# Windowed attention into a SwiGLU block: TensorE's order of work from block 2 on, written out instead of planned

## The chip, the cores and the metric

The kernel runs on one core of a Trainium2 chip. The metric is the device time of one execution in microseconds (us). TensorE is called PE below, VectorE DVE, ScalarE ACT, GpSimd POOL and SyncE SP, as in the profile.

## The reference

The inputs q, k and v have 8 batches, 8 heads, 576 positions and a head size of 64. Attention looks back over a window of 128 positions, with a linear bias per head, and its output, as 4608 tokens of 512 numbers, goes through a gated feed-forward layer with 1536 hidden units.

```python
scores = q @ k.T / sqrt(64)
scores = where((rel >= 0) & (rel < 128), scores - slope[h] * abs(rel), -1e9)
x = softmax(scores) @ v                  # 4608 x 512
out = (silu(x @ w_gate) * (x @ w_val)) @ w_out
```

## The kernel before

Two streams of work share the engines.

**The feed-forward stream** (`ffn`) goes through nine blocks of 512 tokens. In blocks 0 to 5 there are 12 slices m of 128 hidden units, each in two half-steps: the gate product (`pg`, four matmuls of 512 columns, line 398), then ACT's tanh (416) and DVE's `uu` (417); the val product (`pv`, 398), then DVE's `hT` (428). Both take a PSUM bank of the tag `gv`, of which there are three. Blocks 6 to 8 form gate and val from seven products of half size in place of eight (`seven_steps`, line 624), 42 half-steps to a block.

The output projection of block n runs inside block n+1. From block 1 on it is done by `strassen`: two halves t of the columns of tokens, seven products each of six 256-wide matmuls (533), which add up in the two halves X and Y of one bank `po`, and in a bank `p2` for the second product. ACT and DVE copy X and Y out between the products (544 to 576, 537). The set `AT` names the half-steps of a block behind which one such product is written.

The products need sums of quarters of `hT` (`sums`, four DVE operations for each of three chunks c, lines 486 to 489), and of the output weights (`weight_sums`). The seven-step blocks need like sums of the gate and val weights (`gate_val_weight_sums`, 598 to 601) and of the attention output (`x_sums`). `at_once` writes such a list of operations in one go. `later` is a list from which operations are taken off one by one; before the change only the seven-step blocks use it.

**The attention stream** (`attention`) goes through 36 units, nine for each pair of batches. For a unit i it writes:

- `transposes_to`: K and Q transposed, from rank 11 on by DMAs that SP issues;
- `scores(i + 1)`: products of 64 rows (`ps` line 279, `psc` line 314), evicted by ACT with an exponential (285, 318), then multiplied with a mask by DVE (291, 322). One unit's products take all four banks of the tag `a`;
- `weighted(i)`: the product with v (`av`, line 346) in two halves, each in a bank `a`, then DVE's reciprocal and multiply into `x` (348, 349);
- `loads_to` and `ahead`: DMA loads by POOL, some units in advance, and further transposes;
- `x_transposed(i)`: `x` turned into `xT`, up to unit 23 by PE (`px`, line 372) and ACT, later by a DMA. For the units 13 to 23 it is written while the scores of two units on are being written.

Each `yield` of `attention` is one attention step. `ffn` yields sizes (1.0 for a half-step, 0.75 for a product of `strassen`), whose running sum is `step`. Block 2 begins behind step 60, block 6 behind step 198. After each yield of `ffn`, `everything` writes attention steps until their number reaches `target`, and until the units that the block six steps ahead needs are done (`ready`).

**Who sets the order.** A planner orders each engine's instructions by a cost model of its own, except inside `manual_schedule`, where the named engines keep the order of the source. The first tiles are written so for PE, DVE and ACT. From `step >= FIXED_FROM` on it holds for PE alone; the other engines stay with the planner.

Of the kernel before, what the change touches and what calls it, by code (L numbers as in the profile page):

```python
# [19 lines left out]
X_DMA_FROM = 24  # L20
# [11 lines left out]
SEVEN_FROM = 6  # L32
SILU_AT = 7
SECOND = 5.5
RATE = 6.7
FIXED_FROM = 198.0
LATE = 13


# [12 lines left out]
def kernel(  # L52
# [15 lines left out]
    NMB = DFF // P  # L68
# [96 lines left out]
    last = len(units) - 1  # L165
# [318 lines left out]
    def four_sums(a11, a12, a21, a22, s2, s3, s4):  # L484

        return [lambda: nc.vector.tensor_sub(s3, a11, a21),  # L486
                lambda: nc.vector.tensor_add(a21, a21, a22),
                lambda: nc.vector.tensor_sub(s2, a21, a11),  # L488
                lambda: nc.vector.tensor_sub(s4, a12, s2)]

    def at_once(fs):
        for f in fs:
            f()

    def sums(n, c):

        if n not in hsum:
            hsum[n] = [spool.tile([P, HM, 256], FP16, name=f"S{i}", tag=f"S{i}") for i in (2, 3, 4)]
        lo, hi = slice(2 * c, 2 * c + 2), slice(HM + 2 * c, HM + 2 * c + 2)
        a11, a12 = hT[n][:, lo, 0:256], hT[n][:, hi, 0:256]  # L500
        a21, a22 = hT[n][:, lo, 256:512], hT[n][:, hi, 256:512]
        s2, s3, s4 = (t_[:, lo, :] for t_ in hsum[n])
        return four_sums(a11, a12, a21, a22, s2, s3, s4)
# [90 lines left out]
    def gate_val_weight_sums(u):  # L594

        cols = slice(2 * u * P, (2 * u + 2) * P)
        t1, t2, t3, t4 = tsum[u] = t_homes[4 * u:4 * u + 4]
        return [lambda: nc.vector.tensor_sub(t1, V1[:, :, cols], G1[:, :, cols]),
                lambda: nc.vector.tensor_sub(t3, V2[:, :, cols], V1[:, :, cols]),
                lambda: nc.vector.tensor_sub(t2, V2[:, :, cols], t1),  # L600
                lambda: nc.vector.tensor_sub(t4, G2[:, :, cols], t2)]

    def x_sums(n):

        a11, a12 = xT[n][:, 0:HK, 0:256], xT[n][:, HK:NKB, 0:256]
        a21, a22 = xT[n][:, 0:HK, 256:512], xT[n][:, HK:NKB, 256:512]
        s2, s3, s4 = xsum[n] = spare[3 * (n % 2):3 * (n % 2) + 3]
        return four_sums(a11, a12, a21, a22, s2, s3, s4)

    later = []  # L610
# [86 lines left out]
                    of[which[0]][name](which[1])  # L697
                yield n, 7 * u + k, name, which

    AT = {2, 3, *range(5, 10), *range(11, 18)}  # L700

    def ffn():

        for n in range(NBLK):
            if n > 1:
                parts = chain(strassen(n - 1, 0), strassen(n - 1, 1))
            if n == 1:
                for j in range(PRE):
                    for _ in project(0, j, ps_f, "po", 1):
                        yield 1.0  # L710
            if n == SEVEN_FROM:
                break
            for m in range(NMB):
                for half, _ in enumerate(gate_val(n, m)):
                    yield 1.0
                    if n > 1 and 2 * m + half in AT:
                        next(parts)
                        yield 0.75
                if n == 1:
                    if m in (4, 6, 8, 10):  # L720
                        for _ in project(0, m // 2 - 2, ps_f, "po", 1):
                            yield 1.0
                    if m in (4, 6, 8):
                        weight_sums(m // 2 - 2)
                if n > 0 and m >= 9:
                    at_once(sums(n, m - 9))
                if n + 1 == SEVEN_FROM:
                    if m == SILU_AT:
                        attention_ends()
                        by_silu.update((n, i) for i in range(m + 1, NMB))  # L730
                    if m in (SILU_AT + 1, SILU_AT + 2):
                        at_once(gate_val_weight_sums(m - SILU_AT - 1))
                    if m == NMB - 1:
                        at_once(gate_val_weight_sums(2))
                        at_once(x_sums(n + 1))
            if n > 1:
                assert next(parts, 0) == 0
        ends = [strassen(NBLK - 1, t) for t in range(2)]
        final = ()
        for n, k, name, which in seven_steps():  # L740
            if k == 0 and n > SEVEN_FROM:
                assert next(parts, 0) == 0
                parts = chain(strassen(n - 1, 0), strassen(n - 1, 1))
            if n == SEVEN_FROM and k in (3, 10, 17):
                later.extend(gate_val_weight_sums(3 + k // 7))
            yield 0.5
            if k % 3 == 1 and k < 42:
                next(parts)
                yield 0.75
            if k == 20 and n + 1 < NBLK:  # L750
                later.extend(x_sums(n + 1))
            if k == 35:
                later.extend(sums(n, 0))
            if name == "fourth" and which is not None and which[1] > 3:
                if which == (NBLK - 1, 5):
                    at_once(final)
                else:
                    later.extend(sums(which[0], which[1] - 3))
            if n == NBLK - 1 and k == 40:
                final = sums(n, 2)  # L760
                later.append(final.pop(0))
            for _ in range(2 if len(later) > 4 or k >= 39 or k < 7 else 1):
                if later:
                    later.pop(0)()
            if n == NBLK - 1 and k == 41:
                next(ends[0])
                yield 0.75
        assert next(parts, 0) == 0 and not later

        for t in (1, 0, 1, 0, 0, 0, 1, 0, 0, 1, 1, 1, 1):  # L770
            next(ends[t])
            yield 0.75
# [22 lines left out]
    def run(steps):  # L795
        for fs in steps:
            for f in fs:
                f()
            yield
# [34 lines left out]

    def attention():

        waiting = set()
        transposes_to(need[FIRST])
        for _ in run(scores(FIRST)):
            yield FIRST  # L840
        for i in range(FIRST, last + 1):
            behind = LATE <= i < X_DMA_FROM
            if i < last:
                transposes_to(need[i + 1])
                for n, _ in enumerate(run(scores(i + 1))):
                    yield i - (i - 1 in waiting)
                    if n == 2 and i - 1 in waiting:
                        x_transposed(i - 1)
                        waiting.discard(i - 1)
            weighted(i)  # L850
            yield i
            loads_to(i + 7)
            ahead(i)
            yield i
            if behind:
                waiting.add(i)
                yield i
                yield i
                continue
            x_transposed(i)  # L860
            yield i
            yield i + 1
# [63 lines left out]
    def everything():  # L926
        nonlocal done
        base = 0
        busy(WARM)
        with tc.manual_schedule(engines=ENGINES[MANUAL]):  # L930
            first_tiles()
            done = FIRST
            steps = progress(ffn())
            while (at := next(steps)) < ALONE:
                if at == 2.0:
                    nc.scalar.copy(idm2, idm)
                if at in (1.0, 3.0, 4.0):
                    later_masks(2 * (1, 3, 4).index(at) + 2, 2)
        fixed = ExitStack()
        for step in steps:  # L940
            if step >= FIXED_FROM and fixed is not None:
                fixed.enter_context(tc.manual_schedule(engines=ENGINES["pe"]))
                fixed, held = None, fixed
            if step == MASKS_AT:
                make_masks()

            b1 = 24 + 3 * PRE

            lead = LEAD if done < X_DMA_FROM - 2 else LEAD + 4
            blk = (0 if step + LEAD < b1 else 1 if step + LEAD < 60  # L950
                   else min(NBLK - 1, 2 + int((step + lead - 60) // 34.5)))
            if step < b1:

                target = base + 1.25 * max(0, step - ALONE) + 1.5 * max(0, step - 16)
            elif step < 60:
                target = base + 32 + SECOND * 8 * (step - b1) / (60 - b1)
            else:
                target = base + 32 + SECOND * 8 + (step - 60) * RATE * 8 / 34.5
            while (n_att < target or done < ready[blk]) and att_step():
                pass  # L960
        held.close()
# [32 lines left out]
```

The softmax here doesn't subtract the row's maximum and nothing guards it: scores larger than these inputs give would overflow.

## Time and profile before

| | |
|---|---|
| median of 4 runs | 348.69 us (348.07 to 349.44) |
| the profiled execution | 349.44 us |
| its span, first to last instruction | 347.6 us |
| PE busy | 333.9 us (96%) |
| DVE busy | 278.0 us (80%) |
| ACT busy | 207.4 us (60%) |
| granted TensorE clock | 1.000 |

Busy times are unions of the recorded spans. Matmuls are pipelined: the record of one overlaps that of the next, so a PE that is busy all the time can still lose time between matmuls, which shows in the spacing of their starts. The idle time of an engine in front of an instruction is put down to what released it, by its semaphores. A few matmul records are missing.

### The profile page before, as it was taken

The numbers are of one execution on the slowest core, as the hardware profiler recorded it, in microseconds if no ns is written. First come the engines' busy times: TensorE is split into PE (matmuls) and PEld (weight loads), VectorE is DVE, ScalarE is ACT, GpSimd is POOL, SyncE is SP. The second block draws the span as 40 slices with busy tenths as digits, with TensorE's granted clock in tenths as the row PEclk, the third lists the DMA queues.
The fourth block names the chain that finished last, engine by engine and source line by source line (L and its number), as shares of the span: only waits on it lengthen the run. The fifth ranks groups of instructions, "written<-read, shape, count | busy, mean of one in ns | idle before, by whom it ended". The sixth has DMA issues, their size and how long they took to land.

```text
span 347.6 us, 7798 instructions
## 1 busy us (share of the span) xinstructions
PE 333.9 (96%) x2983; PEld 219.3 (63%) x2983; DVE 278.0 (80%) x652; ACT 207.4 (60%) x412; POOL 108.2 (31%) x134
## 2 busy tenths in 40 slices
PE   7999988999999999999999999999999999999995
PEld 4484444454456655566566554566688878878884
DVE  6578885999788699878999799999955875775583
ACT  3758674565655765574754646556467666766750
POOL 8967485257566564536511000000000000000000
PEclk9999999999999999999999999999999999999999
DMA  9999999999999999999994420221201101011014
GB/s 151 170 180 185 142 160 171 109 136 131 140 165 158 181 154 165 155 166 190 151 177 78 75 79 15 32 77 31 78 0 62 62 1 62 2 61 62 1 62 122
DMA packets 158981, 37.37 MB, mean 108 GB/s; under 512 B 147296, under 2 KB 154592, under 8 KB 158944
## 3 DMA queue, kind: packets, MB, share of 16 engines
q0 software_dynamic: 117280, 18.62, 80.5%
q1 hardware_dynamic: 40976, 17.64, 28.7%
q10 hardware_dynamic: 688, 0.62, 0.6%
q8 instruction: 23, 0.38, 0.5%
q14 instruction: 14, 0.11, 0.1%
HBM read 37.91 MB, written 9.44 MB: 136 GB/s over the span
## 4 chain that ended last, share of the span: by engine, by line
PE 63%; DVE 20%; DMA 8%; ACT 4%; issue 3%; POOL 1%; POOLq 0%; ACTq 0%; DVEq 0%
PE po L533 13%; PE pg L398 12%; PE pv L398 11%; PE gX L624 6%; DMA va<-in_v_dram 3%; PE av L346 3%; DMA wo_sb<-in_moe_w_out_dram 3%; PE ps L279 3%; PE gY L624 3%; DVE hT L428 3%; PE p L533 2%; DVE uu L417 2%; DMA qn<-in_q_dram 2%; DVE S L486 2%; PE po L452 2%
## 5 line engine op out<-in xcount | busy, mean ns | idle before, releaser
L398 PE MATMUL pv<-xT,wv_sb 128*128 128x512 f16 (+2 forms) x320 | 76.8, 358 | 0.4 <-DVE hT L428 0.2
L398 PE MATMUL pg<-xT,wg_sb 128*128 128x512 f16 (+2 forms) x320 | 76.2, 358 | 0.5 <-DVE hT L428 0.2
L416 ACT ACTIVATE tt<-pg 128x512 f16<-128x512 f32 (+2 forms) x70 | 41.5, 592 | 40.8 <-PE pg L398 39.4
L285 ACT ACTIVATE ex<-ps 128x512 f16<-128x512 f32 x96 | 50.5, 607 | 16.6 <-PE ps L279 16.5
L417 DVE SCALAR_TENSOR_TENSOR uu<-tt,pg 128x512 f16<-128x512 f16 (+2 forms) x69 | 46.0, 667 | 11.1 <-ACT tt L416 11.0
L428 DVE TENSOR_TENSOR hT<-uu,pv 128x512 f16<-128x512 f16 (+2 forms) x70 | 46.7, 667 | 3.4 <-PE pv L398 1.8
L398 PEld LDWEIGHTS <-wg_sb 128*128 128x128 f16 x320 | 28.5, 98 | 25.2 <-issue 3.3
L398 PEld LDWEIGHTS <-wv_sb 128*128 128x128 f16 x320 | 28.5, 98 | 24.5 <-issue 2.7
L191 POOL DMA_DIRECT2D kn<-in_k_dram x39 | 33.3, 857 | 33.3 <-DMA kT<-kn 24.5
L533 PEld LDWEIGHTS <-hT 128*128 128x128 f16 x384 | 36.5, 98 | 9.2 <-issue 1.1
L185 POOL DMA_DIRECT2D va<-in_v_dram x40 | 34.1, 858 | 22.5 <-PE av L346 15.6
L191 POOL DMA_DIRECT2D qn<-in_q_dram x39 | 33.3, 857 | 23.0 <-DMA qT<-qn 8.6
L291 DVE TENSOR_TENSOR ex<-ex,m_reg 128x1024 f16<-128x1024 f16 x42 | 28.9, 690 | 5.6 <-ACT ex L285 5.4
L533 PEld LDWEIGHTS <-S 128*128 128x128 f16 x288 | 27.3, 98 | 9.3 <-issue 1.8
L349 DVE TENSOR_TENSOR x<-av,rec 128x256 f16<-128x256 f32 x72 | 28.9, 420 | 0.5
L533 PE MATMUL po<-T,S 128*128 128x256 f16 x192 | 26.5, 273 | 1.3 <-DVE S L488 1.0
L533 PE MATMUL po<-T,hT 128*128 128x256 f16 x192 | 26.2, 273 | 0.0
L318 ACT ACTIVATE exc<-psc 128x512 f16<-128x512 f32 x40 | 21.4, 610 | 7.6 <-PE psc L314 7.6
L676 DVE TENSOR_TENSOR hT<-s,v 128x512 f16<-128x512 f16 x18 | 7.6, 424 | 21.4 <-ACT s L675 21.4
L346 PEld LDWEIGHTS <-ex 128*128 128x128 f16 x384 | 17.5, 97 | 5.2 <-issue 0.9
L346 PE MATMUL av<-va,ex 128*128 128x65 f16 x384 | 19.3, 193 | 0.3
L279 PE MATMUL ps<-qT,kT 64*128 64x256 f16 x192 | 18.4, 272 | 0.6 <-DVE osb L537 0.2
(134 smaller groups left out, 538.7 us busy)
## 6 DMA issues: line engine op xcount, KB each, us to landing
out_dram<-osb SPq DMA_DIRECT2D x32, 256.0 KB, 3.5
va<-in_v_dram POOLq DMA_DIRECT2D x32, 128.0 KB, 9.6
qn<-in_q_dram POOLq DMA_DIRECT2D x31, 128.0 KB, 7.4
kn<-in_k_dram POOLq DMA_DIRECT2D x31, 128.0 KB, 7.8
wo_sb<-in_moe_w_out_dram POOLq DMA_DIRECT2D x2, 768.0 KB, 9.3
wg_sb<-in_moe_w_gate_dram POOLq DMA_DIRECT2D x4, 256.0 KB, 8.0
wv_sb<-in_moe_w_val_dram POOLq DMA_DIRECT2D x4, 256.0 KB, 8.4
wg_sb<-in_moe_w_gate_dram POOLq DMA_DIRECT2D x1, 512.0 KB, 9.0
```

The source lines that it names most:

```text
L185: nc.gpsimd.dma_start(va[rank][p0:p1, :, 0:D], src)
L191: nc.gpsimd.dma_start(t_[p0:p1], src)
L285: nc.scalar.activation(e[:, o:o + 2, :], banks[q4][par], AF.Exp, scale=scale)
L291: nc.vector.tensor_mul(e[:, o, :], e[:, o, :], reg[:, o, :])
L346: nc.tensor.matmul(av[:, j, :], w, val, start=(n == 0), stop=(n == len(todo) - 1))
L349: nc.vector.tensor_mul(x[:, 4 * half:4 * half + 4, :], av[:, :, 0:D], rec.broadcast_to([P, 4, D]))
L398: nc.tensor.matmul(ps[:, c0:c1], w[:, kb, ms], xT[n][:, kb, c0:c1], start=(kb == 0 and c0 == 0), stop=(kb == NKB - 1 and c1 == 512), skip_ ...
L416: nc.scalar.activation(tt, pg[:, c0:c1], AF.Tanh, scale=0.5)
L417: nc.vector.scalar_tensor_tensor(out=uu, in0=tt, scalar=one if (n, m) == PIN else 1.0, in1=pg[:, c0:c1], op0=ALU.add, op1=ALU.mult)
L428: nc.vector.tensor_mul(hT[n][:, m, c0:c1], acted[(n, m)][1][:, c0:c1], pv[:, c0:c1])
L533: nc.tensor.matmul(dst, a[:, m, cols], b[:, m, :], start=(start and m == 0), stop=(m == HM - 1), skip_group_check=True)
L624: nc.tensor.matmul(dst[:, i, :], w[:, kb, c0 + i * P:c0 + (i + 1) * P], a[:, kb, :], start=(start and i == 0 and kb == 0), stop=(i == 1 an ...
```

## The change

- `FIXED_FROM` goes from 198.0 to 60: PE follows the source from the end of block 1 on.
- `AT` spreads the 14 products of `strassen` over the half-steps 1 to 22 of a block; before they lay in the half-steps 2 to 17.
- `sums` from the last chunk of block 1 on, `x_sums` and the `gate_val_weight_sums` of block 5 go into `later`. In blocks 2 to 5 one operation is taken off behind each half-step, two when more than three wait. The third of the weight sums moves to block 6, and `x_sums` is queued at slice 7 instead of being written at slice 11.
- `target` behind step 60 becomes 84 + (step - 57) * 54 / 34.5; before it was 76 + (step - 60) * 53.6 / 34.5.
- For units from 13 on, `weighted(i)` is written behind the third step of `scores(i + 1)` instead of behind the last, and `x_transposed` behind the weighted sums of the next unit.

```diff
--- before.py
+++ after.py
@@ -32,8 +32,8 @@
 SEVEN_FROM = 6
 SILU_AT = 7
 SECOND = 5.5
-RATE = 6.7
-FIXED_FROM = 198.0
+RATE = 54.0
+FIXED_FROM = 60
 LATE = 13
 
 
@@ -697,7 +697,7 @@
                     of[which[0]][name](which[1])
                 yield n, 7 * u + k, name, which
 
-    AT = {2, 3, *range(5, 10), *range(11, 18)}
+    AT = {1, 3, 4, 6, 8, 9, 11, 12, 14, 16, 17, 19, 20, 22}
 
     def ffn():
 
@@ -716,6 +716,10 @@
                     if n > 1 and 2 * m + half in AT:
                         next(parts)
                         yield 0.75
+                    if n > 1:
+                        for _ in range(1 + (len(later) > 3)):
+                            if later:
+                                later.pop(0)()
                 if n == 1:
                     if m in (4, 6, 8, 10):
                         for _ in project(0, m // 2 - 2, ps_f, "po", 1):
@@ -723,16 +727,15 @@
                     if m in (4, 6, 8):
                         weight_sums(m // 2 - 2)
                 if n > 0 and m >= 9:
-                    at_once(sums(n, m - 9))
+                    (at_once if n == 1 and m < 11 else later.extend)(sums(n, m - 9))
                 if n + 1 == SEVEN_FROM:
                     if m == SILU_AT:
                         attention_ends()
                         by_silu.update((n, i) for i in range(m + 1, NMB))
                     if m in (SILU_AT + 1, SILU_AT + 2):
-                        at_once(gate_val_weight_sums(m - SILU_AT - 1))
-                    if m == NMB - 1:
-                        at_once(gate_val_weight_sums(2))
-                        at_once(x_sums(n + 1))
+                        later.extend(gate_val_weight_sums(m - SILU_AT - 1))
+                    if m == SILU_AT:
+                        later.extend(x_sums(n + 1))
             if n > 1:
                 assert next(parts, 0) == 0
         ends = [strassen(NBLK - 1, t) for t in range(2)]
@@ -741,8 +744,8 @@
             if k == 0 and n > SEVEN_FROM:
                 assert next(parts, 0) == 0
                 parts = chain(strassen(n - 1, 0), strassen(n - 1, 1))
-            if n == SEVEN_FROM and k in (3, 10, 17):
-                later.extend(gate_val_weight_sums(3 + k // 7))
+            if n == SEVEN_FROM and k in (1, 3, 10, 17):
+                later.extend(gate_val_weight_sums(2 + (k + 4) // 7))
             yield 0.5
             if k % 3 == 1 and k < 42:
                 next(parts)
@@ -834,29 +837,34 @@
 
     def attention():
 
-        waiting = set()
+        waiting = []
         transposes_to(need[FIRST])
         for _ in run(scores(FIRST)):
             yield FIRST
         for i in range(FIRST, last + 1):
-            behind = LATE <= i < X_DMA_FROM
+            late = i >= LATE
             if i < last:
                 transposes_to(need[i + 1])
                 for n, _ in enumerate(run(scores(i + 1))):
-                    yield i - (i - 1 in waiting)
-                    if n == 2 and i - 1 in waiting:
-                        x_transposed(i - 1)
-                        waiting.discard(i - 1)
-            weighted(i)
-            yield i
+                    yield i - len(waiting)
+                    if n == 2 and late:
+                        weighted(i)
+                        yield i - len(waiting)
+            if not late or i == last:
+                weighted(i)
+                yield i
             loads_to(i + 7)
             ahead(i)
-            yield i
-            if behind:
-                waiting.add(i)
+            yield i - len(waiting)
+            if late and i < X_DMA_FROM:
+                if waiting:
+                    x_transposed(waiting.pop(0))
+                waiting.append(i)
                 yield i
                 yield i
                 continue
+            while waiting:
+                x_transposed(waiting.pop(0))
             x_transposed(i)
             yield i
             yield i + 1
@@ -955,7 +963,7 @@
             elif step < 60:
                 target = base + 32 + SECOND * 8 * (step - b1) / (60 - b1)
             else:
-                target = base + 32 + SECOND * 8 + (step - 60) * RATE * 8 / 34.5
+                target = 84 + (step - 57) * RATE / 34.5
             while (n_att < target or done < ready[blk]) and att_step():
                 pass
         held.close()
```

## The prediction

> **What bounds the kernel now.** I read the page first. TensorE (PE) is busy nearly all the time, at full granted clock, so a gain has to come out of the gaps between matmuls.
>
> ```profile
> span 347.6 us, 7798 instructions
> PE 333.9 (96%) x2983; PEld 219.3 (63%) x2983; DVE 278.0 (80%) x652; ACT 207.4 (60%) x412; POOL 108.2 (31%) x134
> DVE  6578885999788699878999799999955875775583
> PEclk9999999999999999999999999999999999999999
> ```
>
> The third and fourth lines are tenths of 40 slices of 8.7 us. DVE (VectorE) stands at 9 from slice 23 to 28, about 200 to 250 us, and lower after. So I looked at blocks 2 to 5, about 103 to 247 us, in windows of 12 us, three to a block; the columns are the window, its length, the busy time of PE, PEld, DVE, ACT, POOL, then clock, DMA share, GB/s.
>
> ```profile
> 127.00:139.00 12.00, 11.94 (x100) 6.41 (x99) 11.64 (x27) 7.60 (x16) 5.64 (x7) 1.00 1.80 155
> 139.00:151.00 12.00, 11.99 (x115) 7.40 (x114) 10.07 (x26) 6.72 (x13) 6.63 (x8) 1.00 2.07 159
> 151.00:163.00 12.00, 12.00 (x111) 7.57 (x109) 8.79 (x19) 7.93 (x17) 5.75 (x7) 1.00 1.60 178
> 163.00:175.00 12.00, 11.51 (x97) 6.29 (x96) 12.00 (x31) 7.32 (x15) 5.76 (x7) 1.00 2.10 169
> 223.00:235.00 12.00, 12.00 (x112) 7.24 (x112) 11.91 (x29) 6.29 (x14) 0.00 (x0) 1.00 0.24 67
> 235.00:247.00 12.00, 11.87 (x116) 7.66 (x116) 11.99 (x35) 6.50 (x13) 0.00 (x0) 1.00 0.30 78
> ```
>
> DVE swings: 8.8 of 12 in mid block 3, 12.0 in its last third, saturated in all of block 5. ACT (ScalarE) is at 58% over the twelve windows (83.6 of 144).
>
> Then PE's waits, first in this stage (103 to 247), then in the stage that is already in source order (247 to 341): total, times, longest.
>
> ```profile
> PE po L533 <- DVE osb L537: 0.5, 2, 0.3
> PE psc L314 <- DVE x L349: 0.5, 1, 0.5
> PE po L533 <- ACT p5s L561: 0.3, 1, 0.3
> PE pg L398 <- DVE hT L428: 0.2, 1, 0.2
> ```
> ```profile
> PE po L533 <- DVE S L488: 1.0, 2, 0.7
> PE gX L624 <- DVE v L667: 0.6, 3, 0.2
> ```
>
> These count only idle time after the modelled end of a pipelined matmul and so understate. The timeline of PE shows the real spacing by its starts:
>
> ```profile
> 164.97 0.61 PE L279 MATMUL ps<-qT,kT 64*128 64x256 f16 x8
> 165.51 0.83 PE L533 MATMUL po<-T,hT 128*128 128x256 f16 x6
> 166.18 1.03 PE L398 MATMUL pg<-xT,wg_sb 128*128 128x512 f16 x4
> 171.37 0.56 PE L314 MATMUL psc<-qT,kT 64*128 64x128 f16 x11
> 172.42 0.39 PE L314 MATMUL psc<-qT,kT 64*128 64x128 f16 x5 [0.49 <-DVE x L349]
> ```
>
> Six 256-wide matmuls take 0.67 from start to next start, 0.109 each; 512-wide ones 0.215; likewise 0.029 for 128x65, 0.055 for 128x128, 0.054 and 0.0275 for the 64-row ones of 256 and 128 columns. The starts from 103.0 on cover 144.2 us with 350, 324, 352, 44, 104 and 112 of these: 75.3 + 35.3 + 10.2 + 2.4 + 5.6 + 3.1 = 131.9. So blocks 2 to 5 hold 12.3 us that are not streaming. I split them by the pair of neighbours: 14 gaps of over 0.16 us make 4.5 (the 0.67 at 171.7 is the largest), and entering a group of 64-row matmuls costs 0.10 before it and up to 0.15 behind it, 0.24 for each of 26 entries, 6.3. The rest, 1.5, is crumbs. From 247 to 340 the same count leaves five gaps, 2.4 us: two on the sums S (1.3), three on v (1.1).
>
> **The change part by part.** No matmul is added or removed; all that can move is the 12.3 us.
>
> *Source order.* (a) The score groups of units 14 to 35 are written as 22 unbroken groups, against 26 entries in the trace: 4 x 0.24 = -1.0. Ends: 0 (others break up) and -1.4 (the two breaks of 0.22 inside groups go too). (b) The waits. What a written order costs here is shown by 247 to 340: without the waits on S, which come of sums in fours before a product, 1.1 in 93 us; over 144 us that is 1.65, and scaled by DVE's share (130.6 of 144 against 63.8 of 93) 2.2. With the waits on S it would be 3.7. I take 2.2, since the change takes the sums one or two per half-step.
>
> *Pacing.* I worked the target formula through by hand. Before, the rule on `ready` pushes attention to count 80 at step 54, the target passes 80 only at step 63, and unit 14's scores come there. After, the target at step 60 is 88.7: nine yields run at once (scores 14 around the weighted sums of unit 13), and from there attention is about 8 steps ahead: unit 20's scores at step 87.25 instead of 95.5, the last unit done at 172.75 instead of 182.5. A step is 1.07 us here (block 2 begins at 101.3, the first seven-step product at 249.4: 148 us for 138 steps). The nine yields cost PE a wait: the first half of the weighted sums needs a bank that the first eviction frees, 0.22 (half the group) + 0.60 after the group's start, while PE is through at 0.43: 0.4. With a tanh (0.49) ahead of it 0.9, and the next group of scores may wait as much: 0.4 to 1.7, I take 0.8 by the nearer row. So waits 4.5 -> 2.2 + 0.8 = 3.0: -1.5.
>
> *Spread products and single sums.* Counted from the order as written, with DVE's back-to-back spacing (0.60 for gate, val and mask, 0.335 for sums and x, 0.09 for rec), a block asks 30 to 34 us of DVE for 34 to 39 of PE. By thirds of blocks the demand over PE's is 0.74, 0.77, 1.09 / 0.68, 0.75, 1.20 / 0.73, 0.78, 1.15 / 0.79, 0.69, 1.26 before, the last third carrying twelve sums (4.0 us) and no products of PE in its last six half-steps. After: 0.82, 0.85, 0.92 / 0.89, 0.80, 0.87 / 1.04, 0.77, 1.00 / 0.92, 0.57, 0.76. This is why I trust (b). One spacing gets tighter: the seventh product of one half and the first of the next are one half-step apart; the copy between them (0.38) lies under a gate of 0.86. Costed at nothing; with a tanh ahead of the copy the cover is gone and it costs 0.1 four times.
>
> *Moved sums.* Eight sums more run in block 6 (2.7 us of DVE) and S of block 5 is written in its steps 1 to 4, used in step 7, 3.3 us later; DVE is at 26.7 of 36 there. Nothing. The waits on S at 281 and 310 belong to blocks 7 and 8, whose order is not touched, and stay.
>
> *Transposes and loads* go with attention: the SP queue and POOL keep their own order. Q of rank 19 landed at 112.9 for scores at 125.5; 8 steps earlier they stand at about 117. Some 4 us are left, so nothing, if the landing keeps its time.
>
> Sum: -1.0 - 1.5 = -2.5 against the profiled execution of 349.4 (span 347.6 and 1.8 around it): 346.9. That execution is 0.75 above the median of the runs, 348.7, so the forecast is **346.2**. Its own ends: every wait and four to six breaks gone, -5.9, 342.8; waits at 3.7 + 1.7 and no groups saved, +0.9, 349.6.
>
> **Two rules of the Trainium skill that speak against it.** The trace: while the group at 171.37 waited for x, the val product behind it did not start. "PSUM — Partial Sum Buffer", section "Engine vs sequencer instructions", says that matmuls start and complete in program order; a row agrees, and by the rule every wait that the writer did not see is paid whole, as in the first rival. The trace: the granted clock is 1.00 in all twelve windows with waits up to 0.67 us. "TensorE: Matmul & The Clock Gate", section "A second HAM failure mode: psum-queue depth-cycling", says that frequent micro-idling can make the clock gate oscillate; by that page's window of 3.4 us, one at half clock would add an estimated 1.7 us. No row here shows it, and the sum leaves it out.
>
> **The rivals.**
> 1. *Slower: weighted sums meet late evictions.* In the new order each weighted group comes a half-step and mostly one product after the next unit's scores, 0.86 + 0.66 us; its second half starts some 0.4 later and needs the second eviction, ready 1.30 after the scores' start, 1.79 with a tanh ahead. About half a microsecond is left. If ACT falls one more slot (0.48) behind, PE waits some 0.35 in each of 22 units: +7.7, 353.9. For it: the order cannot adapt, and banks of `ps_a` are four, all taken by one score group. Against: ACT at 58%. 0.17.
> 2. *Slower: K and Q come late.* The SP queue waits mostly for loads, the DMA share is near 2 until 187 us. If landings slip by more than the 4 us left at units 18 to 20, PE stands 2 to 6 us once: 348 to 352, say 350. 0.08.
> 3. *No change: the scheduled order is nearly the written one already*, or DVE (130.6 of 144) sets the pace: the waits only change names, 348.7. Until unit 20 the trace agrees to 2 us with the written order; in block 5 it does not, unit 35's scores run at 234.8 where the order has them near 224. 0.13.
>
> **How the numbers follow.** The forecast has 0.62. A measurement of this kernel can tell about 0.3%, 1.05 us. Faster by more than that takes waits below some 4.4 us in all with the groups saved: 0.62; within it 0.13; slower 0.25, the two slower rivals. The range takes in the forecast's ends, the second rival and the milder half of the first: 342.8 to 352.0, leaving out about 0.15.
>
> **What would show it.** Right: DVE in windows of 12 us no longer at 12.0 in the last third of a block and below 10 in the second half of block 5; 22 entries into 64-row groups; gaps over 0.16 us from 100 to 247 near 3 us, one of them at scores 14; the last scores some 10 us earlier; the first seven-step product (249.4 now) near 247. Wrong: waits of `av` on evictions of `ps` by the dozen (rival 1), of `ps` on DMA of kT or qT (rival 2), or the same 4.5 us under other names (rival 3).

## The result, and the profile after

The changed kernel takes 347.96 us (median of 46 runs, 347.08 to 348.98) against 349.06 us before (70 runs): a ratio of 0.9973, 95% interval 0.9967 to 0.9980. That is 1.1 us faster; 2.5 us had been forecast. The direction was right, the size was less than half.

The page of the changed kernel, its span, its engines and the rows of DVE and of the granted clock:

```profile
span 346.6 us, 7787 instructions
...
PE 330.0 (95%) x2983; PEld 218.9 (63%) x2983; DVE 277.3 (80%) x652; ACT 207.2 (60%) x412; POOL 108.2 (31%) x134
...
DVE  6578885999798669988899999999855875775583
...
PEclk9999999999999999999999999999999999999999
```

The same work, the same clock. DVE's row is not flatter where it was meant to be: slices 20 to 27 (counted from 0), about 173 to 243 us, all stand at 9. The windows of 12 us (columns as before: length, busy PE, PEld, DVE, ACT, POOL, clock, DMA share, GB/s) say the same:

```profile
127.00:139.00 12.00, 10.90 (x94) 6.22 (x91) 10.31 (x27) 7.30 (x15) 6.49 (x8) 1.00 1.98 145
...
163.00:175.00 12.00, 12.00 (x130) 7.67 (x129) 10.56 (x24) 8.04 (x16) 6.26 (x8) 1.00 2.21 141
175.00:187.00 12.00, 11.99 (x105) 6.91 (x104) 12.00 (x31) 7.39 (x15) 0.89 (x1) 1.00 1.54 209
187.00:199.00 12.00, 11.83 (x108) 7.08 (x106) 11.82 (x30) 6.56 (x13) 0.00 (x0) 1.00 0.24 67
199.00:211.00 12.00, 12.00 (x102) 7.05 (x101) 11.26 (x28) 6.43 (x14) 0.00 (x0) 1.00 0.12 24
211.00:223.00 12.00, 11.21 (x110) 6.69 (x109) 12.00 (x29) 7.29 (x15) 0.00 (x0) 1.00 0.23 67
223.00:235.00 12.00, 11.36 (x116) 7.32 (x114) 12.00 (x32) 6.49 (x12) 0.00 (x0) 1.00 0.21 60
235.00:247.00 12.00, 12.00 (x74) 6.97 (x72) 10.98 (x30) 3.58 (x8) 0.00 (x0) 1.00 0.10 29
```

The last third of block 3 is relieved (10.56 for 12.00), but late block 5 hardly (12.00 and 10.98 for 11.91 and 11.99). PE, on the other hand, now loses busy time in places where it lost almost none: 10.90 from 127 (11.94 before), 11.36 from 223 (12.00 before). PE's waits from 93 to 250 us (total, times, longest) tell on what:

```profile
PE po L533 <- DVE osb L537: 1.9, 3, 1.1
PE psc L314 <- ACT exc L318: 0.8, 1, 0.8
PE p L533 <- ACT ex L285: 0.7, 1, 0.7
PE av L346 <- ACT ex L285: 0.7, 2, 0.5
```

The worst of them, in the timeline of PE and DVE:

```profile
129.40 0.82 PE L533 MATMUL po<-T,S 128*128 128x256 f16 x6
...
130.00 0.68 DVE L417 SCALAR_TENSOR_TENSOR uu<-tt,pg 128x512 f16<-128x512 f16 x1
130.06 1.03 PE L398 MATMUL pg<-xT,wg_sb 128*128 128x512 f16 x4
...
130.71 0.69 DVE L428 TENSOR_TENSOR hT<-uu,pv 128x512 f16<-128x512 f16 x1
...
131.32 0.42 DVE L349 TENSOR_TENSOR x<-av,rec 128x256 f16<-128x256 f32 x1
...
131.74 0.40 DVE L537 SCALAR_TENSOR_TENSOR osb<-po,p5s 128x256 f32<-128x256 f32 x1
...
132.19 0.49 PE L533 MATMUL po<-wo_sb,S 128*128 128x256 f16 x3 [1.10 <-DVE osb L537]
```

The fifth product (`po<-T,S`) is followed one half-step later by the sixth (`po<-wo_sb,S`). They write different halves, X and Y, of one tile of one bank. The sixth waits for DVE's copy of X (`osb<-po,p5s`), and that copy is queued behind `uu`, `hT` and an `x`: it starts at 131.74, while PE had run out of other work at about 130.9. The next product in the written order waits, and with it all that is written behind it.

Counted by the starts of matmuls as in the prediction, but over the whole stage (from the end of block 1's projection at 93.5 or 93.3 to the first seven-step product), the streaming of the matmuls takes 142.6 us in both. Above that lie 13.3 us before and 12.4 after. The gaps of over 0.16 us, called gaps from here on, rose from 5.1 to 6.4 us; the small rest, with the entries into 64-row groups down from 27 to 22, fell from 8.2 to 6.0. The first seven-step product starts at 248.3 instead of 249.4, and everything behind it takes as long as before.

### The profile page after: what moved, and what is told of

Same layout as the page of the kernel before. It is cut to its first block, busy times and chain, and to the rows that moved or that the text cites. A ratio compares the mean times of both kernels' runs of the same rounds, so it can differ in the third digit from the quotient of the medians.

```text
span 346.6 us, 7787 instructions
## 1 busy us (share of the span) xinstructions
PE 330.0 (95%) x2983; PEld 218.9 (63%) x2983; DVE 277.3 (80%) x652; ACT 207.2 (60%) x412; POOL 108.2 (31%) x134
## 4 chain that ended last, share of the span: by engine, by line
PE 55%; DVE 25%; DMA 9%; ACT 5%; issue 4%; POOL 1%; ACTq 0%; DVEq 0%; POOLq 0%
PE po L533 12%; PE pg L398 11%; PE pv L398 9%; PE gX L624 6%; DVE uu L417 3%; DMA wo_sb<-in_moe_w_out_dram 3%; DMA va<-in_v_dram 3%; DVE hT L428 3%; PE gY L624 3%; PE av L346 3%; PE p L533 2%; DVE x L349 2%; DMA qn<-in_q_dram 2%; PE ps L279 2%; DVE ex L291 2%
## 5 line engine op out<-in xcount | busy, mean ns | idle before, releaser
L416 ACT ACTIVATE tt<-pg 128x512 f16<-128x512 f32 (+2 forms) x70 | 41.3, 590 | 53.6 <-PE pg L398 51.8
L279 PE MATMUL ps<-qT,kT 64*128 64x256 f16 x192 | 16.7, 272 | 0.3 <-DVE qT L227 0.2
```

Source lines behind the costliest of these rows:

```text
L416: nc.scalar.activation(tt, pg[:, c0:c1], AF.Tanh, scale=0.5)
```

## The experiments

Each was timed in five rounds against the kernel before on the same chip; the ratios are to that. The last two columns come from each run's trace: the start of the first seven-step product, and the gaps of over 0.16 us in the stage before it. A trace is of one execution: that of e5 was 1.1 us below its median, that of e1 0.9 and that of e4 0.7. The stage does not begin at the same time in all of them either: the last matmul ahead of it starts at 92.9 us in the changed kernel, at 91.8 in e1 and at 91.9 in e5. So the ratios carry the verdicts and the last columns only the places.

| kernel | ratio (95% interval) | first seven-step product, us | gaps, us |
|---|---|---|---|
| before | 1 | 249.4 | 5.1 |
| changed | 0.9973 (0.9967 to 0.9980) | 248.3 | 6.4 |
| source order alone (e2) | 1.0100 (1.0082 to 1.0118) | 252.9 | 10.7 |
| changed, planner's order (e3) | 0.9945 (0.9926 to 0.9963) | 246.8 | 3.6 |
| changed, old places of products (e4) | 1.0039 (1.0024 to 1.0054) | 249.7 | 8.5 |
| the same, planner's order (e11) | 0.9996 (0.9982 to 1.0010) | 248.8 | 5.2 |
| changed, old pace (e5) | 1.0029 (1.0015 to 1.0042) | 248.9 | 7.9 |
| the same, planner's order (e10) | 0.9959 (0.9944 to 0.9975) | 247.4 | 3.8 |
| changed, sums in fours (e6) | 0.9991 (0.9976 to 1.0006) | 248.5 | 6.3 |
| changed, sixth product apart (e1) | 0.9953 (0.9935 to 0.9971) | 246.5 | 5.8 |
| changed, other bank for p2 (e7) | 0.9947 (0.9931 to 0.9963) | 246.7 | 5.5 |
| planner's order, sixth apart (e9) | 0.9938 (0.9917 to 0.9959) | 245.8 | 3.8 |
| changed, both repairs (e8) | 0.9896 (0.9878 to 0.9913) | 245.0 | 3.2 |
| planner's order, both repairs (e12) | 0.9891 (0.9873 to 0.9909) | 244.7 | 2.7 |

Theory A: what a written order costs is set by where it puts a product in front of a bank that another engine still has to read. Theory B: VectorE is full, and waits taken away in one place come back in another.

**e2, source order alone**, on the kernel before.

```diff
-FIXED_FROM = 198.0
+FIXED_FROM = 60
```

> The kernel before with TensorE in source order from step 60, nothing else. Theory A: the old places of the products (one half-step between nearly all of them) and the sums in fours make the fixed order meet more shared banks: waits of 8 to 12 us in blocks 2 to 5, 353 us, ratio 1.01. Theory B, or that the source order is good by itself as the prediction had it: 346 to 349, ratio 0.993 to 1.0.

It is 3.5 us slower, and the gaps double to 10.7 us. The first rows of its waits, and one of them in the timeline, where a sixth and a seventh product stand one half-step apart:

```profile
PE po L533 <- DVE osb L537: 1.9, 4, 1.0
PE po L533 <- ACT p5s L561: 1.0, 3, 0.3
PE ps L279 <- ACT ex L285: 0.9, 2, 0.6
PE psc L314 <- DVE x L349: 0.6, 1, 0.6
```
```profile
123.94 0.82 PE L533 MATMUL po<-wo_sb,S 128*128 128x256 f16 x6
124.60 1.03 PE L398 MATMUL pv<-xT,wv_sb 128*128 128x512 f16 x4
126.60 0.81 PE L533 MATMUL po<-T,hT 128*128 128x256 f16 x6 [0.98 <-DVE osb L537]
```

So the source order by itself is a loss; the prediction had it as the gain.

**e3, everything but the source order.**

```diff
-FIXED_FROM = 60
+FIXED_FROM = 198.0
```

> The changed kernel with the planner's order on TensorE up to block 6 as before: spread products, pacing and single sums alone. Theory A: the planner puts products elsewhere, so waits stay near 4.5 us, and the even sums are worth little: 348 to 349, ratio 0.997 to 1.0. Theory B (the even demand on VectorE is what was gained): 347.5 to 348, ratio 0.996.

0.9945, better than the changed kernel by 1.0 us, and better than either theory had it; the two intervals do not overlap. Of the 6.4 us of gaps 3.6 are left. PE's waits:

```profile
PE po L533 <- DVE osb L537: 0.8, 3, 0.4
PE p L533 <- ACT ex L285: 0.4, 1, 0.4
PE ps L279 <- PE po L533: 0.3, 1, 0.3
```

The first two rows are of the same kinds, smaller: in front of the sixth product at 131.62 and of the second at 120.91 the planner has put matmuls of a val product, which the written order has behind them. The third row names PE itself, which had long been done; what it waited for is open. The gain of the change lies wholly in its other parts, and the order gives part of it back.

**e4 and e11, the old places of the products**, in source order and in the planner's.

```diff
-    AT = {1, 3, 4, 6, 8, 9, 11, 12, 14, 16, 17, 19, 20, 22}
+    AT = {2, 3, *range(5, 10), *range(11, 18)}
```

> The changed kernel with the products of the output projection back in the old half-steps 2 to 17. Theory A: more products one half-step behind one that VectorE has to read (third to seventh of both halves), waits of po on osb at twice the changed kernel's 2.8 us: 350.5, ratio 1.004. Theory B: VectorE's demand is uneven again, but its sum the same: 348 to 349, ratio 0.998 to 1.0.

> The planner's order up to block 6, new pacing, single sums, but the products in the old half-steps 2 to 17. If the places gain apart from the source order: 0.998 to 1.0. If the planner moves the products anyway, and they gain only in source order: 0.9945.

1.0039 and 0.9996. Spreading the products is worth 0.66% (2.3 us) in source order and 0.51% (1.8 us) in the planner's; the planner does not make up for the bunching. In e4 the waits of `po` on the copies are the largest row by far, against 1.9 in the changed kernel:

```profile
PE po L533 <- DVE osb L537: 3.1, 5, 0.8
```

**e5 and e10, the old target line**, in source order and in the planner's.

```diff
-                target = 84 + (step - 57) * RATE / 34.5
+                target = 76 + (step - 60) * 6.7 * 8 / 34.5
```

> The changed kernel with the old target line behind step 60 (76 at step 60, no burst, attention some 7 steps later). Theory A (waits at places of the written order decide): the two waits of the burst, 1.0 us, go; attention ends 8 us later but its demand is spread the same: 347.0 to 348.0, ratio 0.994 to 0.997. Theory B (attention done earlier is what was gained, since VectorE is full at the end of block 5): 349 to 350, ratio 1.0 to 1.002.

> The planner's order up to block 6, spread products, single sums, but the old target line. If the pacing is what gains apart from the source order: 0.999 to 1.001. If it gains only by mending the source order: 0.9945 as with the new line.

In source order the new pace is worth 0.56% (2.0 us). Theory A had expected a small gain from losing the burst at step 60 and missed; theory B has the side right, and the time is a little beyond its figure. The waits are the usual kinds at other places, and PE loses most from 223 to 235, with attention still going on and DVE full:

```profile
223.00:235.00 12.00, 10.58 (x115) 6.57 (x113) 11.93 (x31) 5.64 (x12) 0.00 (x0) 1.00 0.23 67
```

In the planner's order the pace gives 0.14%, with overlapping intervals: unclear. So the pace mainly mends the source order, as one of the two expectations of e10 had it (its 0.9945 lies inside the interval).

**e6, the sums of the hidden units in fours.**

```diff
-                    (at_once if n == 1 and m < 11 else later.extend)(sums(n, m - 9))
+                    at_once(sums(n, m - 9))
```

> The changed kernel with the sums of the hidden units taken in fours again at slices 9 to 11, the sums of weights and of x still singly. Theory A: twelve sums stand before the copies out of po in the last third of a block, where the new places have three products: waits of po on osb from 2.8 to 4 or 5 us: 349.5, ratio 1.001. Theory B (only the total demand counts): as the changed kernel, 348, ratio 0.997.

0.9991 against 0.9973, with intervals that overlap; the gaps are 6.3 against 6.4 us and nearly the same ones. Unclear, some 0.6 us if anything; theory A's 4 to 5 us on `osb` did not come. The singly taken sums of weights and of `x`, and the new places of `weighted` and `x_transposed`, were not tried alone.

**e1, the sixth product two half-steps behind the fifth.**

```diff
-    AT = {1, 3, 4, 6, 8, 9, 11, 12, 14, 16, 17, 19, 20, 22}
+    AT = {1, 3, 4, 6, 7, 9, 11, 12, 14, 15, 17, 18, 20, 22}
```

> The changed kernel with three products moved by one half-step (8 to 7, 16 to 15, 19 to 18), so that the sixth product of a half comes two half-steps after the fifth. Theory A (the sixth product writes the bank whose other half VectorE still has to read after the fifth, and the written order leaves one half-step for that): the waits of po on osb, 2.8 us in the changed kernel's trace, go to below 0.8; 2 us faster than the changed kernel, 346.0, ratio to before 0.991. Theory B (VectorE is full, so the waits come back in front of other instructions): 347.5 to 348.5, ratio 0.996 to 0.998.

0.9953, 0.7 us better than the changed kernel by the ratios, whose intervals overlap by a hair; between the two theories. The waits of the sixth product (2.8 us by starts) are gone altogether, as theory A had it, but the time fell by less. Some of it came back elsewhere, and one new wait is the second rival of the prediction:

```profile
142.19 0.82 PE L533 MATMUL po<-T,S 128*128 128x256 f16 x6
143.51 0.99 PE L279 MATMUL ps<-qT,kT 64*128 64x256 f16 x8 [0.50 <-PE po L533]
```

The row names PE itself, which had long been done. One of the DMA transposes of q, issued at 136.1, landed at 143.6, when the eight score products started to run. In the changed kernel the same transpose landed at 142.9, 2.2 us ahead of its scores. A wait for v of 0.36 at 107.7 is of the same sort.

**e7, another bank for the second product.** `p2` used to take one of the four banks that the scores fill.

```diff
-            p2 = (ps_f.tile([P, HC], FP32, name="p2", tag="gv") if seeded
-                  else ps_a.tile([P, HC], FP32, name="p2", tag="a"))
+            p2 = ps_f.tile([P, HC], FP32, name="p2", tag="gv")
```

> The changed kernel with the second product's bank taken from the three of gate and val instead of the four of the scores, in all blocks. Theory A (the second product meets banks that the scores have just filled): the waits of p and of psc on evictions, 0.9 + 0.25 + 1.0 us, go, and gate and val with two banks for a while give back less than 1: 346.5, ratio 0.993. Theory B: gate and val have no bank to spare with VectorE full, and the waits come back as pg and pv on uu and hT: 348 to 350, ratio 0.998 to 1.003.

0.9947, 0.9 us better than the changed kernel, between the two theories and nearer to A's 0.993; the intervals do not overlap. Its waits hold no row of `p` or `psc` any more; instead there is one of `pg`, 0.8 us, and one for v, while the row of `po` stays:

```profile
PE po L532 <- DVE osb L536: 1.8, 3, 1.1
PE pg L398 <- DVE uu L417: 0.8, 2, 0.5
PE av L346 <- ACT ex L285: 0.7, 2, 0.5
PE av L346 <- DMA va<-in_v_dram: 0.4, 1, 0.4
```

**e8, e9 and e12, the repairs together, and with the planner's order.**

> The changed kernel, source order kept, with both repairs: sixth products two half-steps behind the fifth, and the second product's bank from those of gate and val. Theory A (the written order loses by what it puts in front of full banks, and each repair takes its own waits away): the gains of the two runs add, -0.7 and -0.9: 346.5 against 349.1 before, ratio 0.9927, level with the planner's order. Theory B (one limit behind both, the queue on VectorE or late q, k and v): no more than the better of the two, ratio 0.995.

> The changed kernel with the planner's order up to block 6 and the sixth products two half-steps behind the fifth. Theory A: the planner's order without the waits of po on osb (1.4 us in the planned run's trace): 346.0, ratio 0.991. Theory B: the planner moves the products anyway, so their written places hardly count: 347, ratio 0.9945 as in the planned run.

> The planner's order up to block 6 with both repairs. Theory A: another 0.6 us less than with the moved sixth products alone (the waits of p, 0.37 and 0.25, and of psc, 0.24): ratio 0.992. Theory B: the bank taken from gate and val gives as much back: 0.994.

The two repairs of e1 and e7 together, in source order, give 0.9896, 3.6 us faster than before and 2.7 faster than the changed kernel: more than the two gains added (1.6 us), and beyond what theory A expected. The gaps are halved, 3.2 us for 6.4. PE's waits are down to these:

```profile
PE av L346 <- ACT ex L285: 0.7, 2, 0.5
PE pg L398 <- DVE uu L417: 0.5, 1, 0.5
PE po L532 <- DVE osb L536: 0.4, 1, 0.4
PE ps L279 <- DVE x L349: 0.2, 1, 0.2
```

In the planner's order the first repair alone (e9) shows no difference clear of the intervals: 0.9938 against the 0.9945 of e3, as theory B had it, where theory A had 0.991. The waits of the sixth product are gone from its trace (1.35 us by starts in e3), but a wait of 0.65 for the same late q and one of 0.60 in front of a seventh product stand in their place. Both repairs (e12) give 0.9891, better than theory A's 0.992, which the intervals do not tell from e8. Once the full banks are out of the way, no difference between the two orders is measured. DVE is as full in e8 as in the changed kernel, in its windows of 12 us:

```profile
175.00:187.00 12.00, 12.00 (x109) 7.32 (x107) 12.00 (x30) 7.05 (x15) 0.89 (x1) 1.00 1.70 204
211.00:223.00 12.00, 11.47 (x118) 7.18 (x118) 12.00 (x30) 6.83 (x15) 0.00 (x0) 1.00 0.13 27
```

So theory B, as a bound that no place can change, is out. These two are the best versions found.

## Why the prediction was right or wrong

**Faster, by moving gaps and nothing else: right in direction, by luck.** The same matmuls run in every version, 142.6 us of streaming in the stage; all that moved is what lies between them. But the source order, which was to bring the gain together with the pacing, cost 1.0 us, and the places of the products, put at nothing, more than made up for it.

**The score groups: right in kind, too small.** 22 unbroken groups were forecast and are there. The part of the loss that is not waiting fell by 2.2 us, where 1.0 had been put down: five entries fewer at 0.24 make 1.2, the spacing inside the groups gave 0.5, and most of the rest only changed its name, as two more groups than before end in a gap that is counted as a wait.

**The waits of the source order, step (b): wrong, and the step that failed.** It sized them by the rate of the stage behind 249 us, scaled with DVE's share: 2.2 us without the burst. Measured: 6.4, of which the burst is 1.0, so 5.3 in place of 2.2 (4.9 from 103 us on, where the prediction counted). That stage was no fair yardstick: its gate and val products accumulate in tiles `gX`, `gY` and `gZ` with a bank each, its products of `strassen`, which share `po` there too, start 1.96 us apart, and no attention takes banks between them. In blocks 2 to 5 X and Y share a bank that DVE reads (2.8 us of waits), and `p2` shares its four banks with scores that fill them all (1.2 on `p`, 1.0 on `psc`). e1 and e7 take away just these. The banks were in the code and the prediction named four of them under its first rival; it priced a share of DVE and not a place in the order. Its upper bound of 3.7, with the waits on S, was left unscaled; scaled by DVE's share like the 2.2 it is 4.9, near the measured figure, but by waits on S that do not occur here. Source order costs 1.0 us with the change's other parts and 3.5 without them.

**The burst at step 60: right in price, from a count that was off.** 1.0 us, between 0.4 and 1.7, with 0.8 taken. The count gave the units with two score sets three attention steps instead of five. So the number at step 54 is 84 and not 80, the burst is five yields and not nine, the target line of before passes that number at step 65, and the last unit's weighted sums are written near step 182 instead of near 190, where `attention_ends` wrote out what was left. The lead of some 8 steps survives: the last group of scores starts 8.6 us earlier (226.20 for 234.83), its last matmul 9.5. Block 2 also begins at 95.4 in the trace of before, not at 101.3. By the corrected count unit 35's scores stand at step 184 in the order of before, an estimated 234 us at 1.12 us a step from 95.4 on, so that the trace (234.8) agrees with the written order in block 5 too; what the third rival said against this is wrong. None of it made the size wrong.

**Spread products and pacing: the sign of their worth was missed.** They were costed at nothing and used as a reason to trust (b). They are the gain, as far as the parts were tried: 1.8 us for the places in the planner's order, and in source order 2.3 for the places and 2.0 for the pace. The pair that was called tight, the seventh product and the next half's first, shows no large wait. The one that mattered, fifth and sixth, is left out of it; the table of demand by thirds looked even, and that was the reason given to trust (b). An even demand per third says nothing on a queue of 1.7 us (130.00 to 131.74) in front of one copy.

**Moved and single sums: nothing, as forecast,** as far as e6 can tell.

**Transposes and loads: no wait in the changed kernel, as forecast, but the 4 us were not there.** The forecast left 4 us for the transposes of q; the changed kernel has 2.2 for one of them. With other waits gone, e1 meets its landing with 0.66 us to wait, and e7 one of v with 0.59. In e8 that transpose was issued 1.2 us earlier than in e1 and landed at 141.7, ahead of its scores at 142.4, and that v landed at 106.8 instead of 108.4. What made them earlier is not shown; the stage itself begins 0.8 us later in e8's trace than in e1's, so a part may lie in the execution and not in the edit.

**DVE's windows: half right.** Under 12.0 in the last third of a block was forecast and came: 10.31, 10.56, 11.26 and 10.98 in blocks 2 to 5. Under 10 in the second half of block 5 did not come (12.00 and 10.98), and the full windows moved forward, into the first third of block 4 and the first two of block 5: the queue stays filled up to 235 us.

**The rules of the Trainium skill.** That matmuls start in program order is seen at 132.19, where the sixth product holds the whole queue; it speaks for the loss, as cited. The clock gate that micro-idling may set off does not show: 1.00 in all twelve windows with 6.4 us of gaps. A third rule lies behind the rows here. "PSUM — Partial Sum Buffer", section "PSUM bank collisions raise a hardware error", says to guard PSUM by bank and quadrant, or simply by bank, and not by address. The half-bank waits of `po` fit that. One place in the changed kernel's own trace shows the other case. In the last projection the code gives X and Y a tile and a bank each, and there the sixth product starts right behind the fifth, while DVE copies X:

```profile
340.51 0.82 PE L533 MATMUL po<-T,S 128*128 128x256 f16 x6
...
341.19 0.82 PE L533 MATMUL po<-wo_sb,S 128*128 128x256 f16 x6
341.37 0.42 DVE L537 SCALAR_TENSOR_TENSOR osb<-po,osb 128x256 f32<-128x256 f32 x1 [0.23 <-PE po L533]
```

So the pair waits where it shares a tile in one bank. Whether the tile or the bank makes it wait is not shown, and neither a bank each in blocks 2 to 5 nor an earlier copy on DVE was tried.

## What to carry to other kernels

Before an order is fixed by hand, list for each product the bank it writes, who reads that bank last, and how long that reader's queue is at this point; keep such pairs two slots apart, and give a short-lived accumulator a bank that no burst fills. Do not size the waits of a new order by a stage with another layout of banks, nor by the busy share of an engine. Try each part of a bundled change alone: here the part that gave it its name cost time, and the places of the products, in source order with the pace, carried the gain.

## What was not expected of the hardware

Entering a group of 64-row matmuls between 128-row ones costs PE about 0.24 us each time, 0.10 before it and up to 0.15 behind it. DVE, working without a pause, takes 0.60 us from start to start for a `uu` or `hT` recorded as 0.68, and 0.335 for a sum or an `x` recorded as 0.42, so sums of recorded durations overstate its load by a seventh to a quarter.
